# Two pairs of row-sum accumulators, and a row-sum matmul that stands one unit later

## The chip, the cores and the metric

The kernel runs on one core of a Trainium2 chip. A core has five engines with a queue each: TensorE (PE in the profile, with its weight loads as PEld), VectorE (DVE), ScalarE (ACT), GpSimd (POOL) and SyncE (SP), which here issues nearly all DMAs. An engine takes its own instructions in order and waits for others by semaphores. The metric is the device time of one launch in microseconds (us), as the median of several runs.

## The reference

The reference is four layers on one sequence of 2048 rows of 1024: attention, spectral filter, attention, spectral filter, each with a layer norm and a residual.

```python
def _A_ref(x, wqkv, wo):                     # H = 32 heads of Dh = 32
    qkv = (x @ wqkv).reshape(B, S, 3, H, Dh).transpose(2, 0, 3, 1, 4)
    q, k, v = qkv[0], qkv[1], qkv[2]
    scores = jnp.einsum("bhqd,bhkd->bhqk", q, k) * (Dh ** -0.5)
    p = softmax(scores, axis=-1)
    o = jnp.einsum("bhqk,bhkd->bhqd", p, v)
    return o.transpose(0, 2, 1, 3).reshape(B, S, D) @ wo
def _B_ref(x, w_r, w_i):
    X = rfft2(x) * (w_r + 1j * w_i)
    return irfft2(X, s=(S, D))
x = x + _A_ref(layernorm(x), wqkv, wo)
x = x + _B_ref(layernorm(x), w_r, w_i)
x = x + _A_ref(layernorm(x), wqkv, wo)
x = x + _B_ref(layernorm(x), w_r, w_i)
```

## The kernel before

**Attention.** The 32 heads are handled as 8 groups `g` of 4 heads. The loop of line 626 runs over the groups, over 4 chunks `c` of 512 queries, and over 16 key tiles `kt` of 128 keys. One step (g, c, kt) is called a unit here, and the step from kt = 15 to kt = 0 of the next chunk a chunk boundary; there are 32 chunks in each of the two attention layers.

A unit has these parts. `S` (line 552) makes the scores of 4 heads by 12 matmuls in two tiles `s` of PSUM, from a pool of three such tiles, and ScalarE turns each of them into a tile `p` of exponentials (line 562; a pool of 8 tiles). `PV` (line 564) multiplies them with V into the PSUM tile `o`; it is called at even kt for the two units before. `add` (line 575) sums the exponentials over the key tiles on VectorE, into two accumulators `acc` of 128x1024 in f32: at kt = 0 it does nothing, at kt = 1 one instruction (line 579) writes the sum of the tiles of kt = 0 and kt = 1, and from then on line 581 adds to it. So two VectorE instructions of 128x1024 belong to each unit but those of kt = 0.

`add` runs behind: the units whose PV was just issued are in `late`, and one of them is added in each of the next two units. So the last key tile of a chunk (kt = 15) is added in the unit kt = 1 of the next chunk. Right behind that stands `fin` (line 583): 4 matmuls with a matrix of ones (line 587, "the row-sum matmul" here) sum `acc` over the 128 partitions into a tile `z`, which is one of the three `s` tiles. VectorE then makes the reciprocal of it and scales the output: transpose (588), reciprocal (590), maximum into a flag (591), transpose (593), product with `oc` (594). These five are called the z instructions. At kt = 5, `out` (line 597) splits the scaled output in two f16 parts and SyncE writes it to memory.

**What sets the order.** Inside `tc.manual_schedule` (line 625) TensorE and ScalarE take their instructions in the order in which the code issues them. VectorE's and GpSimd's order, and that of the DMAs, comes from the scheduler of the framework, which sorts them by its own estimate of when they are ready.

**Filler.** Between the units of odd kt and the next, TensorE gets a piece of other work: the projections of the next groups (`qk_chunk`, line 340; `v_tiles`, line 384) or parts of the output projection (line 443). A chunk of Q or K that is complete is split by ScalarE and VectorE (lines 167 and 168), squared (344), and after four chunks `norms` (line 351) sums the squares by a small matmul (357) into another of the three `s` tiles, which VectorE reduces (359).

**Spectral layer.** `spectral` ends with 16 steps of a transpose (965), a matmul (977) and additions to x: three VectorE instructions a step (`sd` 987, and 988 and 989 into x) and one on GpSimd for two steps (992). In the first spectral layer the weights of the next attention layer are loaded beside it and split by VectorE (line 168, into `wv` and `wqk`). Line 958 opens the small pools of attention again, in memory that the constants and work tiles of the spectral layer held.

**Memory.** `acc` lies in a large tile `R` (line 203), of which attention has parts free. `open_small` (line 212) opens the pools of the attention layers one behind the other: a pool that is put in moves the addresses of those behind it.

Of the kernel before, what the change touches and what calls it, by code (L numbers as in the profile page):

```python
# [6 lines left out]
F32 = mybir.dt.float32  # L7
# [5 lines left out]
ALU = mybir.AluOpType  # L13
# [157 lines left out]
def run(g):  # L171
    for _ in g:
        pass


class Pools:
    def __init__(self, tc, side):
        self.tc, self.side, self.ctx = tc, side, ExitStack()
# [10 lines left out]
class AttnPools:  # L189


    def __init__(self, tc):
        self.tc = tc
        self.low = Pools(tc, "left")
        self.big = self.low("at_x", 1).tile([128, 16384], F32, name="big")
        self.right = Pools(tc, "right")
        r = self.right("at_r", 1).tile([128, 16384], F32, name="R")
        self.x = r.rearrange("p (t d) -> p t d", d=1024)
        k = r.bitcast(F16).rearrange("p (t a n) -> p t a n", a=2, n=2048)
        self.k = [k[:, i] for i in (3, 4, 5)]  # L200
        self.q = k[:, 2]
        v = r.rearrange("p (a t c) -> p a t c", t=16, c=128)
        self.v = [v[:, i] for i in (0, 1, 6)]
        a = r.rearrange("p (a j n) -> p a j n", j=2, n=512)
        self.acc = [a[:, i] for i in (14, 15)]

    def close(self):
        self.small.close()
# [3 lines left out]
    def open_small(self):  # L212
        small = self.small = Pools(self.tc, "left")
        self.pp = small("at_p", 8)
        self.qp = small("at_q", 1)
        self.oc = small("at_oc", 1)
        self.sgp = small("at_stage", 3)
        self.wqp = small("at_wqk", 2)
        self.wvp = small("at_wv", 1)
        self.sq = small("at_sq", 1)  # L220
        self.on = small("at_on", 2)
        self.on2 = small("at_on2", 2)
        self.sm = small("at_sm", 2)
        self.stages = [(self.sgp, "wst")] * 3 + [(self.on, "zt")] * 2 + [(self.on2, "ohl")] * 2
# [45 lines left out]
def attention(nc, tc, layer, ap, xin, yd, wts, wo, cst, dram, flags):  # L270
# [6 lines left out]
    small, psum = ap.small, Pools(tc, None)  # L277
# [118 lines left out]
    def sums(ph):  # L396
        return 8 if ph[0] == "v" else 4

    def filler():
        run(prep(phases[0]))  # L400
        for i, ph in enumerate(phases):
            nxt = prep(phases[i + 1]) if i + 1 < len(phases) else iter(())
            for n in range(sums(ph)):
                yield from (v_tiles if ph[0] == "v" else qk_chunk)(ph, n)
                for _ in range(1 + (n > 0)):
                    next(nxt, None)
            run(nxt)
# [6 lines left out]
    def load_wo():  # L414
        st = []

        def load(i):
            if i < 16:
                s = sgp.tile([128, 512], F32, name="wst")
                nc.sync.dma_start(s, wo[i // 2 * 128:i // 2 * 128 + 128, i % 2 * 512:i % 2 * 512 + 512])  # L420
                st.append(s)
        load(0)
        load(1)
        for i in range(16):
            load(i + 2)
            d, sl = i // 2, slice(i % 2 * 512, i % 2 * 512 + 512)
            split(nc, wo_t[0][d // 4][:, d % 4, sl], wo_t[1][d // 4][:, d % 4, sl], st[i], SW)
            yield
# [54 lines left out]
    def wo_parts():  # L483
        load_o(0)
        load_o(1)
        for t in [2, 3, 0, 1] + list(range(4, 12)):
            if t == 8:
                two = wvp.tile([128, 2, 1024], F32, name="wv")
                wo_dst[8], wo_dst[9] = two[:, 0], two[:, 1]
            yield from wo_part(t // 4, t % 4, wo_dst[t])  # L490
            if t in (1, 7):
                load_o(t // 4 + 2)
# [54 lines left out]
    both.clear()  # L547


    P, O, acc = {}, {}, ap.acc  # L550

    def S(g, c, kt):

        s = [psS.tile([128, 2, 512], F32, name="s") for _ in range(2)]
        for i, (a, b) in enumerate(((0, 0), (0, 1), (1, 0))):
            for h in range(4):
                r = slice(32 * h, 32 * h + 32)
                nc.tensor.matmul(s[h // 2][:, h % 2], K[g][r, a, kt * 128:kt * 128 + 128],  # L558
                                 Q[g][r, b, c * 512:c * 512 + 512], start=i == 0, stop=i == 2)
        for hf in range(2):  # L560
            p = P[g, c, kt, hf] = pp.tile([128, 2, 512], F32, name="p")
            nc.scalar.activation(p, s[hf], AF.Exp, bias=bias[g], scale=SCALE / (SQ * SQ))  # L562
# [12 lines left out]
    def add(g, c, kt):  # L575
        for hf in range(2):
            p = P[g, c, kt, hf]
            if kt == 1:
                nc.vector.scalar_tensor_tensor(acc[hf], P[g, c, 0, hf], 1e-34, p, op0=ALU.add, op1=ALU.add)  # L579
            elif kt:  # L580
                nc.vector.tensor_add(acc[hf], acc[hf], p)  # L581

    def fin(g, c):
        zt = on.tile([128, 16, 32], F32, name="zt")
        z = psS.tile([128, 2, 512], F32, name="s")[:, 0]
        for h in range(4):
            nc.tensor.matmul(z[32 * h:32 * h + 32], cst["ones"], acc[h // 2][:, h % 2], start=True, stop=True)  # L587
        nc.vector.transpose(zt.rearrange("p a b -> p (a b)"), z)
        rc = sm.tile([128, 16], F32, name="rc")
        nc.vector.reciprocal(rc, zt[:, :, 0])  # L590
        nc.vector.tensor_max(flags["r"], flags["r"], rc)
        r = on.tile([128, 512], F32, name="zt")
        nc.vector.transpose(r.rearrange("p (a b) -> p a b", b=32), rc.unsqueeze(2).broadcast_to([128, 16, 32]))
        nc.vector.scalar_tensor_tensor(r, O[g, c], SO, r, op0=ALU.mult, op1=ALU.mult)
        O[g, c] = r
# [8 lines left out]
        else:  # L604
            olast[c] = t

    pend, done, late = [], [], []
    fill, lwo, wof = filler(), load_wo(), wo_parts()
    left, parts, rests = 16, 20, list(range(12))

    def slots(f, sums, n, steps):

        while sums:
            k = max(1, int(n / sums + 0.5))
            m = -(-steps // k)
            for i in range(0, steps, m):
                while left_norms:
                    norms()
                for _ in range(min(m, steps - i)):
                    next(f, None)  # L620
                n -= 1
                yield sums - (i + m >= steps)
            sums -= 1

    with tc.manual_schedule(engines={mybir.EngineType.PE, mybir.EngineType.Activation}):
        for g in range(NG):
            todo = sum(sums(ph) for ph in beside.get(g, []))
            sl = slots(fill, todo, 22 if g == NG - 2 else 32, 24)
            wsl = slots(wof, 4, 10, 21)
            for u in range(NCH * NKT):  # L630
                c, kt = divmod(u, NKT)
                S(g, c, kt)
                if kt % 2 == 0:
                    for w in pend:
                        PV(*w)
                    late = pend
                    pend = []
                for w in late[:1]:
                    add(*w)
                    if w[2] == NKT - 1:  # L640
                        fin(*w[:2])
                        done = [w[:2]]
                late = late[1:]
                if kt == 5 and done:
                    out(*done.pop())
                pend.append((g, c, kt))
                if kt % 2 == 0:
                    continue
                if todo:
                    todo = next(sl)  # L650
                elif g == NG - 2:
                    if left:
                        run(lwo)
                        left = 0
                    if next(wsl, None) is not None and u == NCH * NKT - 1:
                        run(wsl)
                elif g == NG - 1:
                    t = rests[0] if rests else 16
                    if (t // 4 < c - 1 or t // 4 == c - 1 and kt >= 7) and (kt % 4 == 3 or not parts):
                        wo_rest(rests.pop(0))  # L660
                    elif parts:
                        parts -= 1
                        for _ in range(21):
                            next(wof)
                if g == NG - 2 and todo < 4:
                    for _ in range(2):
                        if left > (8 if todo == 3 else 0):
                            next(lwo, None)
                            left -= 1
        for w in pend:  # L670
            PV(*w)
        for w in late + pend:
            add(*w)
        run(wof)
        for t in rests:
            wo_rest(t)
# [560 lines left out]
```

## Time and profile before

| | |
|---|---|
| median of 3 runs | 3885.8 us (3885.0 to 3886.59) |
| the profiled execution's own time | 3887.92 us |
| its span, first to last instruction | 3886.0 us |
| granted TensorE clock, mean | 0.988 |
| TensorE busy | 3738.1 us (96%), 32951 instructions |
| VectorE busy | 3181.9 us (82%), 3967 instructions |
| ScalarE busy | 2901.1 us (75%), 3567 instructions |
| GpSimd busy | 304.1 us (8%), 386 instructions |
| row-sum matmul, first to last start | 175.9 to 3583.1 us |

A group row of the profile reads: line, engine, operation, what it writes <- what it reads, shape, count, then busy us in all, mean ns of one, idle us of the engine just before, and what ended that idle time. A row of the timeline reads: start us, length us, engine, line, operation, tiles, shape, how many were merged, and in brackets the engine's idle time ahead of it and what ended it. The end of a matmul is modelled, so the distance between two starts tells more of TensorE than its length. Each f32 matmul of lines 568 and 587 leaves two records. A window row reads: the stretch, its length, busy us (instructions), granted clock, share of the DMA engines, GB/s.

### The profile page before, as it was taken

The page shows a single profiled execution, that of the slowest core. Times are in us where ns is not written, and L with a number is a line of the kernel's source. Part 1 is how long each engine was busy: PE and PEld are TensorE (multiplying, and loading weights), DVE is VectorE, ACT ScalarE, POOL GpSimd, SP SyncE. Part 2 cuts the span into 40 slices and gives each one's busy share as a digit, 9 for nine tenths or more (in the row PEclk, how much of TensorE's full clock was granted, in tenths as well). Part 3 has the DMA queues.
Part 4 walks back from the last instruction along what each step waited for, and adds up shares of the span by engine and source line. Part 5 has one row for each costly group of instructions (what it writes and reads, how often), then busy time and mean ns, then how long its engine had stood idle before and what let it go on. Part 6 is the DMA issues. An engine that isn't in the chain of part 4 may idle for free.

```text
span 3886.0 us, 79635 instructions
## 1 busy us (share of the span) xinstructions
PE 3738.1 (96%) x32951; PEld 1644.2 (42%) x32951; DVE 3181.9 (82%) x3967; ACT 2901.1 (75%) x3567; POOL 304.1 (8%) x386
## 2 busy tenths in 40 slices
PE   6999999999999999989989999999999999999998
PEld 4322433343234233368854334333433432333788
DVE  6689899989998987966675998989899889788544
ACT  4578887888788865657855888888888888666686
POOL 1000000000000000014320000000000000000143
PEclk9999999999999999999999999999999999999999
DMA  8000000000000221134270000000000002111333
GB/s 204 15 12 23 12 12 17 18 12 18 12 26 7 73 70 64 62 142 140 62 179 12 15 23 12 12 18 18 12 20 12 23 12 90 53 69 66 147 99 105
DMA packets 165575, 194.08 MB, mean 50 GB/s; under 512 B 74961, under 2 KB 120657, under 8 KB 164177
## 3 DMA queue, kind: packets, MB, share of 16 engines
q1 hardware_dynamic: 164912, 188.82, 15.6%
q8 instruction: 260, 4.26, 0.5%
q14 instruction: 115, 0.93, 0.1%
q10 hardware_dynamic: 288, 0.07, 0.0%
HBM read 123.83 MB, written 48.23 MB: 44 GB/s over the span
## 4 chain that ended last, share of the span: by engine, by line
PE 73%; DVE 12%; issue 7%; ACT 3%; DMA 3%; POOL 1%; SPq 0%; DVEq 0%; ACTq 0%; POOLq 0%
PE o L568 20%; PE s L558 17%; PE x L340 12%; PE x L384 7%; PE x L443 6%; DVE R L581 3%; ACT p L562 2%; PE ps L862 2%; PE ps L800 2%; PE s L587 1%; PE ps L791 1%; DMA w<-in_w 1%; PE s L443 1%; PE o L384 1%; PE ps L977 1%
## 5 line engine op out<-in xcount | busy, mean ns | idle before, releaser
L562 ACT ACTIVATE p<-s,bias 128x1024 f32<-128x1024 f32 x2048 | 2169.7, 1112 | 575.4 <-PE s L558 564.5
L581 DVE TENSOR_TENSOR R<-R,p 128x1024 f32<-128x1024 f32 x1792 | 2089.0, 1218 | 139.4 <-ACT p L562 136.3
L568 PE MATMUL o<-p,R 128*32 128x512 f32 x8192 | 985.5, 599 | 0.0
L340 PE MATMUL x<-big,wqk 128*128 128x512 f16 x2880 | 684.2, 383 | 17.0 <-DVE Q L168 6.3
L558 PEld LDWEIGHTS <-R 32*128 32x128 f16 x12288 | 233.0, 92 | 769.3 <-issue 654.3
L340 PEld LDWEIGHTS <-wqk 128*128 128x128 f16 x3072 | 277.3, 98 | 452.9 <-issue 159.1
L558 PE MATMUL s<-Q,R 32*128 32x512 f16 x6144 | 433.0, 378 | 12.0 <-ACT p L562 10.7
L558 PE MATMUL s<-R 32*128 32x512 f16 x6144 | 432.3, 379 | 8.2 <-ACT p L562 6.7
L568 PEld LDWEIGHTS o<-p,R 128*32 128x32 f32 x8192 | 213.8, 109 | 524.6 <-issue 524.0
L384 PEld LDWEIGHTS <-big 128*128 128x128 f16 x3072 | 296.5, 100 | 155.5 <-issue 73.9
L384 PE MATMUL x<-wv,big 128*128 128x256 f16 x2688 | 324.1, 277 | 34.5 <-DMA big<-hl 34.5
L579 DVE SCALAR_TENSOR_TENSOR R<-p 128x1024 f32<-128x1024 f32 x128 | 153.9, 1203 | 196.1 <-ACT p L562 195.7
L443 PE MATMUL x<-big 128*128 128x512 f16 x1050 | 237.4, 380 | 0.0
L365 POOL PARTITION_ALL_REDUCE mall<-mqk x16 | 40.7, 2542 | 2333.8 <-DVE mqk L359 2322.5
L443 PEld LDWEIGHTS <-big 128*128 128x128 f16 x1344 | 126.2, 98 | 178.0 <-issue 34.6
L910 DVE TENSOR_TENSOR H<-G,H 128x512 f16<-128x512 f32 (+1 forms) x68 | 46.5, 683 | 105.4 <-ACT H L909 105.3
L862 PE MATMUL ps<-cbi,H 128*128 128x256 f16 (+1 forms) x792 | 99.2, 273 | 6.0 <-ACT H L909 3.7
L855 ACT COPY U<-ps 64x256 f32<-64x256 f32 (+1 forms) x272 | 97.2, 357 | 8.4 <-PE ps L862 3.3
L855 ACT COPY B<-ps 64x256 f32<-64x256 f32 (+1 forms) x272 | 97.1, 357 | 6.7 <-PE ps L862 2.4
L862 PE MATMUL ps<-cb,big 128*128 128x256 f16 x780 | 96.3, 273 | 0.0
L805 DVE TENSOR_TENSOR big<-ps,big 128x512 f16<-128x512 f32 x64 | 44.5, 695 | 58.5 <-ACT big L804 58.5
L167 ACT ACTIVATE R<-x 128x512 f16<-128x512 f32 x88 | 52.7, 598 | 50.5 <-PE x L340 50.4
(429 smaller groups left out, 2992.5 us busy)
## 6 DMA issues: line engine op xcount, KB each, us to landing
wst<-in_wp SPq DMA_DIRECT2D x96, 256.0 KB, 3.0
R<-y SPq DMA_DIRECT2D x32, 512.0 KB, 5.4
w<-in_w SPq DMA_DIRECT2D x60, 256.0 KB, 2.7
od<-ohl SPq DMA_DIRECT2D x56, 256.0 KB, 2.4
big<-od SPq DMA_DIRECT2D x16, 896.0 KB, 6.7
y<-R SPq DMA_DIRECT2D x20, 512.0 KB, 2.7
R<-in_x SPq DMA_DIRECT2D x16, 512.0 KB, 5.8
wst<-in_wo SPq DMA_DIRECT2D x32, 256.0 KB, 3.0
```

Source lines behind the costliest of these rows:

```text
L167: nc.scalar.activation(hi, src, AF.Copy, scale=scale)
L340: nc.tensor.matmul(ps, a, b, start=d == 0 and i == 0, stop=d == 7 and i == 2)
L384: nc.tensor.matmul(ps[:, j], l, r, start=d == 0 and i == 0, stop=d == 7 and i == 2)
L443: nc.tensor.matmul(p, a, b, start=start and d == ds[0] and i == 0, stop=stop and d == ds[-1] and i == 2)
L558: nc.tensor.matmul(s[h // 2][:, h % 2], K[g][r, a, kt * 128:kt * 128 + 128], Q[g][r, b, c * 512:c * 512 + 512], start=i == 0, stop=i == 2)
L562: nc.scalar.activation(p, s[hf], AF.Exp, bias=bias[g], scale=SCALE / (SQ * SQ))
L568: nc.tensor.matmul(O[g, c][32 * h:32 * h + 32], V[g][:, kt, 32 * h:32 * h + 32], P[g, c, kt, h // 2][:, h % 2], start=kt == 0, stop=kt == ...
L579: nc.vector.scalar_tensor_tensor(acc[hf], P[g, c, 0, hf], 1e-34, p, op0=ALU.add, op1=ALU.add)
L581: nc.vector.tensor_add(acc[hf], acc[hf], p)
L800: nc.tensor.matmul(pa[:, j], tt[:, j], mm[:, g], start=True, stop=True)
L855: nc.scalar.copy(ov[64 * r:64 * r + 64, a0:a0 + m, x], tl[64 * x:64 * x + 64, :m, r])
L862: nc.tensor.matmul(out, l, r, start=k == 0, stop=k == len(mm_) - 1)
```

## The change

Even chunks keep the accumulators in `R`. Odd chunks get a second pair, `acc1`, in a new pool of 8 KB a partition that opens behind `at_p`. The last `add` of a chunk no longer calls `fin`; it leaves the chunk in `full`, and `fin` is called in the unit kt = 2, behind the `PV` calls for kt = 0 and kt = 1. `out` stays at kt = 5. Memory that the program reserves for DMA descriptors is set to 4096 bytes a partition.

```diff
@@ class AttnPools
-        self.acc = [a[:, i] for i in (14, 15)]
+        self.acc0 = [a[:, i] for i in (14, 15)]
@@ def open_small
         self.pp = small("at_p", 8)
+        self.accp = small("at_acc", 1)
         self.qp = small("at_q", 1)
@@ def attention
-    P, O, acc = {}, {}, ap.acc
+    P, O = {}, {}
+    acc1 = ap.accp.tile([128, 2, 2, 512], F32, name="acc")
+    acc = [ap.acc0, [acc1[:, i] for i in range(2)]]
@@ def add
         for hf in range(2):
             p = P[g, c, kt, hf]
+            t = acc[c % 2][hf]
             if kt == 1:
-                nc.vector.scalar_tensor_tensor(acc[hf], P[g, c, 0, hf], 1e-34, p, op0=ALU.add, op1=ALU.add)
+                nc.vector.scalar_tensor_tensor(t, P[g, c, 0, hf], 1e-34, p, op0=ALU.add, op1=ALU.add)
             elif kt:
-                nc.vector.tensor_add(acc[hf], acc[hf], p)
+                nc.vector.tensor_add(t, t, p)
@@ def fin
-            nc.tensor.matmul(z[32 * h:32 * h + 32], cst["ones"], acc[h // 2][:, h % 2], start=True, stop=True)
+            nc.tensor.matmul(z[32 * h:32 * h + 32], cst["ones"], acc[c % 2][h // 2][:, h % 2], start=True, stop=True)
@@ the loop over units
-    pend, done, late = [], [], []
+    pend, done, late, full = [], [], [], []
...
                     late = pend
                     pend = []
+                    if kt == 2 and full:
+                        done = [full.pop()]
+                        fin(*done[0])
                 for w in late[:1]:
                     add(*w)
                     if w[2] == NKT - 1:
-                        fin(*w[:2])
-                        done = [w[:2]]
+                        full = [w[:2]]
@@ def kernel
-    nc = _bacc.Bacc("TRN2", target_bir_lowering=False, num_devices=1)
+    nc = _bacc.Bacc("TRN2", target_bir_lowering=False, num_devices=1, dynamic_dma_scratch_size=4096)
```

What it moves is shown at three places. In the changed kernel the lines are 561 for S, 571 for PV, 591 for the row-sum matmul, 341 for the filler, 583 and 585 for the sums, 592 to 598 for the z instructions and 993 to 995 for the spectral additions.

TensorE at the start of chunk 1 of group 2, second attention layer (`s` is the scores, `x` the filler's sum); before, the row-sum matmul stands between the last matmul of S of kt = 1 and the filler:

```order
L558 MATMUL s<-R 128x512
L587 MATMUL s<-R,ones 32x512 x4
L340 LDWEIGHTS wqk
L340 MATMUL x<-big,wqk 128x512
L340 LDWEIGHTS wqk
```

and now, with the 8 matmuls of the two PV of unit kt = 2 ahead of it:

```order
L561 MATMUL s<-R 128x512
L571 MATMUL o<-p,R 32x512 x8
L591 MATMUL s<-R,ones 32x512 x4
L561 LDWEIGHTS R
L561 MATMUL s<-R 128x512
```

It moved behind the filler, S of kt = 2 and the 8 matmuls of PV, and S of kt = 3 follows it. The three `s` tiles are taken in turn, so the tile of `z` is next wanted by S of kt = 4, where before it was wanted by S of kt = 3.

VectorE at the same boundary, before (`zt` and `rc` belong to the z instructions, line 168 and 344 are the split and the square of a chunk of K):

```order
L579 SCALAR_TENSOR_TENSOR R<-p 128x1024
L588 STREAM_TRANSPOSE zt<-s 128x512
L579 SCALAR_TENSOR_TENSOR R<-p 128x1024
L590 RECIPROCAL rc<-zt 128x16
L168 SCALAR_TENSOR_TENSOR R<-x,R 128x512
L591 TENSOR_TENSOR fr<-fr,rc 128x16
L593 STREAM_TRANSPOSE zt<-rc 128x512
L344 TENSOR_TENSOR sq<-R 128x512
L594 SCALAR_TENSOR_TENSOR zt<-oc,zt 128x512
L581 TENSOR_TENSOR R<-R,p 128x1024 x8
```

and now at the same boundary (the chunk that begins is odd, so its sums go to `acc`; the first row is its sum of kt = 0 and kt = 1, both halves):

```order
L583 SCALAR_TENSOR_TENSOR acc<-p 128x1024 x2
L168 SCALAR_TENSOR_TENSOR R<-x,R 128x512
L345 TENSOR_TENSOR sq<-R 128x512
L585 TENSOR_TENSOR acc<-acc,p 128x1024 x2
L592 STREAM_TRANSPOSE zt<-s 128x512
L594 RECIPROCAL rc<-zt 128x16
L595 TENSOR_TENSOR fr<-fr,rc 128x16
L597 STREAM_TRANSPOSE zt<-rc 128x512
L598 SCALAR_TENSOR_TENSOR zt<-oc,zt 128x512
L585 TENSOR_TENSOR acc<-acc,p 128x1024 x6
```

The five z instructions stand together now, behind the additions of kt = 2; before, other instructions lay between them. Nothing else of VectorE's order in the attention loops moved, but that at six boundaries the reduction of line 359 stands ahead of the first sum of the chunk.

VectorE at the end of the first spectral layer, before (`wv` and `wqk` are the weights being split):

```order
L987 TENSOR_TENSOR sd<-e,ps 128x512
L989 TENSOR_TENSOR R<-R,ps 128x16x8x4
L168 SCALAR_TENSOR_TENSOR wv<-wst,wv 128x4x128
L988 TENSOR_TENSOR R<-R,ps 128x16x8x4
L987 TENSOR_TENSOR sd<-e,ps 128x512
L989 TENSOR_TENSOR R<-R,ps 128x16x8x4
L168 SCALAR_TENSOR_TENSOR wv<-wst,wv 128x4x128
L168 SCALAR_TENSOR_TENSOR wqk<-wst,wqk 128x512
L987 TENSOR_TENSOR sd<-e,ps 128x512
L988 TENSOR_TENSOR R<-R,ps 128x16x8x4
L168 SCALAR_TENSOR_TENSOR wqk<-wst,wqk 128x512
```

and now:

```order
L993 TENSOR_TENSOR sd<-e,ps 128x512
L995 TENSOR_TENSOR R<-R,ps 128x16x8x4
L168 SCALAR_TENSOR_TENSOR wv<-wst,wv 128x4x128 x2
L993 TENSOR_TENSOR sd<-e,ps 128x512
L994 TENSOR_TENSOR R<-R,ps 128x16x8x4
L168 SCALAR_TENSOR_TENSOR wqk<-wst,wqk 128x512
L995 TENSOR_TENSOR R<-R,ps 128x16x8x4
L994 TENSOR_TENSOR R<-R,ps 128x16x8x4
L993 TENSOR_TENSOR sd<-e,ps 128x512
L995 TENSOR_TENSOR R<-R,ps 128x16x8x4
L168 SCALAR_TENSOR_TENSOR wqk<-wst,wqk 128x512
```

The splits of weights moved against the steps: the new pool shifts the tiles that the loads go to, so they wait for other work. A GpSimd addition (line 992, now 998) starts behind every second step's `sd`. ScalarE's order differs at one such split, and those of GpSimd and SyncE are the same; some of their waits name other engines.

## Prediction

> **What bounds the kernel now.** I read the page first: busy shares, then the chain of work that ended last. In each of the two rows the reader should look at how far TensorE stands above VectorE.
>
> ```profile
> PE 3738.1 (96%) x32951; PEld 1644.2 (42%) x32951; DVE 3181.9 (82%) x3967; ACT 2901.1 (75%) x3567; POOL 304.1 (8%) x386
> PE 73%; DVE 12%; issue 7%; ACT 3%; DMA 3%; POOL 1%; SPq 0%; DVEq 0%; ACTq 0%; POOLq 0%
> ```
>
> TensorE is busy for 96% of the span and carries 73% of the chain; VectorE carries 12% of it, so there are stretches where VectorE sets the pace. Next come the groups of instructions, for the two lines around the change:
>
> ```profile
> L579 DVE SCALAR_TENSOR_TENSOR R<-p 128x1024 f32<-128x1024 f32 x128 | 153.9, 1203 | 196.1 <-ACT p L562 195.7 <-PE s L587 0.5
> L587 PE MATMUL s<-R,ones 128*32 128x512 f32 x512 | 73.9, 604 | 1.6 <-DVE R L581 1.4 <-ACT p L562 0.2
> ```
>
> VectorE's idle time ahead of the first sum of a chunk is 195.7 us on ScalarE's exponentials and only 0.5 us on the row-sum matmul. That is the first warning: the write-after-read wait which a second pair of accumulators takes away costs VectorE almost nothing. The row-sum matmul runs 64 times, 73.9 us in all. An undisturbed one, at 2485.02 below, shows 1.06, and 64 of those are 67.8; so TensorE lost 6.1 us inside and 1.6 ahead, 7.7 us in all, by waiting for the last additions. Then the timeline at one quiet boundary (chunk 1 of group 2, second attention layer), where the reader follows the starts of TensorE and of VectorE:
>
> ```profile
> 2484.26 0.83 PE L558 MATMUL s<-R 32*128 32x512 f16 x12
> ...
> 2485.02 1.06 PE L587 MATMUL s<-R,ones 128*32 128x512 f32 x8
> ...
> 2486.01 1.90 PE L340 MATMUL x<-big,wqk 128*128 128x512 f16 x8
> 2486.27 1.23 DVE L579 SCALAR_TENSOR_TENSOR R<-p 128x1024 f32<-128x1024 f32 x1 [2.04 <-ACT p L562]
> 2487.41 0.71 DVE L588 STREAM_TRANSPOSE zt<-s 128x512 f32<-128x512 f32 x1
> ...
> 2487.85 0.83 PE L558 MATMUL s<-R 32*128 32x512 f16 x12
> ...
> 2488.05 1.18 DVE L579 SCALAR_TENSOR_TENSOR R<-p 128x1024 f32<-128x1024 f32 x1
> 2488.60 1.92 PE L568 MATMUL o<-p,R 128*32 128x512 f32 x16
> ...
> 2489.15 0.24 DVE L590 RECIPROCAL rc<-zt 128x16 f32<-128x16 f32 x1
> 2489.31 0.63 DVE L168 SCALAR_TENSOR_TENSOR R<-x,R 128x512 f16<-128x512 f32 x1
> ...
> 2489.86 0.16 DVE L591 TENSOR_TENSOR fr<-fr,rc 128x16 f32<-128x16 f32 x1
> 2489.93 0.70 DVE L593 STREAM_TRANSPOSE zt<-rc 128x512 f32<-128x512 f32 x1
> ...
> 2490.46 0.83 PE L558 MATMUL s<-R 32*128 32x512 f16 x12
> 2490.56 0.38 DVE L344 TENSOR_TENSOR sq<-R 128x512 bf16<-128x512 f16 x1
> 2490.86 0.68 DVE L594 SCALAR_TENSOR_TENSOR zt<-oc,zt 128x512 f32<-128x512 f32 x1
> ...
> 2491.46 9.16 DVE L581 TENSOR_TENSOR R<-R,p 128x1024 f32<-128x1024 f32 x8
> ```
>
> TensorE has no gap here; the row-sum matmul takes 0.99 from its start to the next one, and no wait stands in brackets on TensorE. VectorE waits 2.04 for exponentials and then works without a pause. At other boundaries TensorE does wait:
>
> ```profile
> 726.83 2.35 DVE L581 TENSOR_TENSOR R<-R,p 128x1024 f32<-128x1024 f32 x2
> 728.19 2.09 PE L587 MATMUL s<-R,ones 128*32 128x512 f32 x8 [0.56 <-DVE R L581]
> 729.34 1.23 DVE L579 SCALAR_TENSOR_TENSOR R<-p 128x1024 f32<-128x1024 f32 x1 [0.16 <-PE s L587]
> ...
> 732.79 0.69 DVE L168 SCALAR_TENSOR_TENSOR R<-x,R 128x512 f16<-128x512 f32 x1 [0.33 <-ACT R L167]
> ```
>
> The matmul starts 0.56 late and then its second half waits for the second addition, 1.03 more (2.09 against 1.06). I went through all 64 in this way: seven waits make up the 7.7 us, six in the first attention layer. What matters is what VectorE does next. For each boundary I took the stretch from its first sum to the next place where TensorE waits for VectorE, or to where VectorE runs dry, and asked for VectorE's busy time. For 22 boundaries the stretch ends in a TensorE wait; first, last and sum are:
>
> ```profile
> 177.20:200.80 23.60, 23.52 (x28) 1.00 0.04 12
> ...
> 3250.60:3291.50 40.90, 40.76 (x50) 0.96 0.49 162
> sum 545.70, DVE 540.52; mean DVE 24.57
> ```
>
> VectorE is busy 540.52 of 545.70 us, 99%. So at these 22, to which all seven boundaries belong, VectorE is the bound until the stretch ends; a wait of TensorE that is removed at its start is met again at its end.
>
> **The change, part by part.** Profiled execution and median stand 2.1 us apart (3887.9 against 3885.8); I make the sum against the profiled one and subtract it from the median alike.
>
> *The waits at the old place.* 7.7 us go there and come back behind, but for what VectorE itself idled: 0.16 and 0.33 in the rows above, at the three boundaries where it idles so (the others show none), 0.49 x 3 = 1.5. **-1.5** (ends: 0, and -7.7 if all stays gone).
>
> *The matmul joins a run of PV.* Alone, 8 records take 0.99. PV's 16 records of the same kind take 2490.46 - 2488.60 = 1.86, eight more than the 0.99 of eight alone: the second eight cost 0.87, so joining a run saves 0.12. It is worth something where TensorE is the bound: 64 matmuls, of which 2 stand behind the last chunk of a layer and are not moved, less 22, is 40. **-4.8** (ends: 0 and 62 x 0.12 = -7.4).
>
> *The reduction of norms.* At six boundaries a small matmul follows that takes the next `s` tile:
>
> ```profile
> 317.90 1.07 PE L587 MATMUL s<-R,ones 128*32 128x512 f32 x8
> 319.17 0.40 PE L357 MATMUL s<-sq,bones 128*32 128x512 bf16 x4 [0.20 <-ACT p L562]
> ```
>
> It starts 1.27 behind the row-sum matmul in place of 0.99, as the tile is still being read by ScalarE. With `z` gone from there it gets the tile that `z` had: 0.28 x 6. **-1.7** (ends: 0, and -1.7).
>
> *VectorE's order.* The five z instructions stand in a row now. Before, others lay between, and a row's start came ahead of the end of the one before: 2488.05 is 0.07 ahead of 2487.41 + 0.71. Neighbours of which one needs the other's result do not overlap so:
>
> ```profile
> 826.15 0.70 DVE L593 STREAM_TRANSPOSE zt<-rc 128x512 f32<-128x512 f32 x1
> 826.89 0.69 DVE L594 SCALAR_TENSOR_TENSOR zt<-oc,zt 128x512 f32<-128x512 f32 x1
> ```
>
> The second starts 0.04 behind the end of the first. At 2487.41 the five took, start to next start, 0.64 + 0.16 + 0.07 + 0.63 + 0.60 = 2.10. In a row I take 0.75 + 0.28 + 0.07 + 0.74 + 0.60 = 2.44, the durations plus 0.04 at the three dependent neighbours: 0.34 more. That is free where VectorE has slack and whole where it is the bound, at 22: **+7.5** (ends: 0, and 22 x 0.46 = +10.1 if the fourth pair waits too). [...]
>
> *The buffer.* `z` leaves the `s` pool later; S of kt = 4 wants its tile, before S of kt = 3. Counting from S of kt = 1 at 2484.26, TensorE now runs S 0.76, filler 1.84, S 0.75, PV 1.86, z 0.87, S 0.75, filler 1.84: S of kt = 4 is wanted at +8.67. VectorE's first sum starts at +2.01; two sums 2.3, split 0.6, square 0.3, two additions 2.3 (row 726.83), transpose 0.71: the tile is free at +8.2. Half a microsecond of room. **0** in the forecast; its failing is rival C.
>
> *End of the first spectral layer.* The new pool moves addresses, and splits of weights change places against GpSimd's additions. A split that meets one is slow:
>
> ```profile
> 1925.63 0.67 DVE L168 SCALAR_TENSOR_TENSOR wv<-wst,wv 128x512 f16<-128x512 f32 x1
> 1928.42 3.10 POOL L992 TENSOR_TENSOR R<-R,sd 128x1024 f32<-128x1024 f32 x1 [13.90 <-DVE sd L987]
> 1928.86 3.21 DVE L168 SCALAR_TENSOR_TENSOR wv<-wst,wv 128x512 f16<-128x512 f32 x1
> ...
> 1947.90 2.02 PE L977 MATMUL ps<-mi,tt 128*128 128x128 f32 x16 [1.12 <-DVE R L988]
> ```
>
> 3.21 against 0.67, 2.5 each. Three stand behind such a start before and two now; TensorE waits for VectorE there only 1.12. I take half. **-1.3** (ends: 0 and -2.5).
>
> *More accumulators, smaller descriptor memory, later loads:* no instruction is added, and SyncE's order is the same; 0.
>
> The sum is -1.5 - 4.8 - 1.7 + 7.5 - 1.3 = **-1.8**: 3886.1 on the profiled execution, 3884.0 against the median.
>
> **The rivals.** *A, VectorE does not bound those stretches:* the seven waits go for good and the chain of z costs nothing: -7.7 - 4.8 - 1.7 - 1.3 = -15.5, 3870.3. The 73.9 in the group row speaks for it; the 99% against.
>
> *B, the row of z instructions costs nothing:* if VectorE's next row waits for the last one's end in any case, the forecast less 7.5, 3876.5. For it: within the chain of the trace only one dependent pair of neighbours could be read. Against: its row. [...]
>
> *C, the end on the other side: `z` holds its `s` tile too long.* If one more addition (1.22) gets ahead of the transpose, the tile comes free at +9.4, and with ScalarE's exponentials behind S pushed too, S of kt = 4 waits 0.7 to 1.1, say 0.9. The boundaries where filler of Q and K adds a split and a square to VectorE are about 20 of the 40: +18 on the forecast, 3902 (3894 to 3910). It decides as soon as the transpose ends later than 8.67 behind S of kt = 1. For it: half a microsecond is small beside the 2.04 by which VectorE's start depends on exponentials. Against: in the order only the two additions of kt = 2 precede it.
>
> **How the numbers follow.** Forecast 0.60, A 0.10, B 0.12, C 0.18. The likeliest one is 3884.0; its own range is 3877 to 3894, the first with the VectorE term at 0, the second with TensorE's gains at 0 and VectorE's at its upper end (3885.8 + 10.1 - 1.5, rounded). What a measurement of this kernel can tell from no change is about 0.2%, 7.8 us: 3878.0 to 3893.6. The forecast lies within it, A and B are faster, C slower: faster 0.22, same 0.60, slower 0.18. For 8 in 10 the range takes in B with 2 us below it and the cheaper part of C: 3874 to 3900; A and the dearer part of C, about 0.10 each, are left out.
>
> **What would show it.** In the changed profile the row-sum matmul's row should fall from 73.9 to about 62 with no idle on VectorE's additions, while TensorE's waits on line 168's, 345's and 359's results in the first attention layer grow by about as much as went. The product with `oc` should start 0.04 behind the end of its transpose; if ahead, B. S of kt = 4 with a wait on a z transpose in brackets means C, and busy VectorE well under 99% in the 22 stretches means A. What would make all of it wrong is a wait that I haven't seen in TensorE's order: the row-sum matmul itself now stands ahead of S of kt = 3, so if VectorE's last addition ends behind PV, every exponential behind it is late.

## The result and the profile after

| | before | changed |
|---|---|---|
| median of 20 runs each | 3886.3 us (3882.0 to 3893.3) | 3889.0 us (3883.1 to 3893.7) |
| ratio | | 1.0004, 95% interval 0.9998 to 1.0011 |
| the profiled execution's span | 3886.0 us | 3888.7 us |
| TensorE busy | 3738.1 us | 3726.9 us |
| VectorE busy | 3181.9 us | 3192.0 us |

The ratio is +1.6 us, between -0.8 and +4.3: no change that this measurement can tell, where -1.8 was forecast. The page of the changed kernel, busy times first, then the groups that answer to those shown of before (the row-sum matmul has two rows now, one for each pair), with the two on which TensorE waits for VectorE:

```profile
PE 3726.9 (96%) x32951; PEld 1649.8 (42%) x32951; DVE 3192.0 (82%) x3967; ACT 2897.0 (74%) x3567; POOL 304.3 (8%) x386
L341 PE MATMUL x<-big,wqk 128*128 128x512 f16 x2880 | 685.0, 384 | 24.5 <-DVE Q L168 11.2 <-DVE R L168 5.6 <-ACT wqk L167 5.4
L591 PE MATMUL s<-acc,ones 128*32 128x512 f32 x256 | 33.4, 593 | 0.0
L591 PE MATMUL s<-R,ones 128*32 128x512 f32 x256 | 33.3, 592 | 0.0
L358 PE MATMUL s<-sq,bones 128*32 128x512 bf16 x128 | 18.9, 391 | 17.3 <-DVE sq L345 16.0 <-POOL sq L345 1.0 <-ACT p L565 0.4
```

and the two waiting groups of the kernel before, which the prediction did not show:

```profile
L340 PE MATMUL x<-big,wqk 128*128 128x512 f16 x2880 | 684.2, 383 | 17.0 <-DVE Q L168 6.3 <-ACT wqk L167 5.4 <-DVE R L168 3.2
L357 PE MATMUL s<-sq,bones 128*32 128x512 bf16 x128 | 15.6, 389 | 10.7 <-DVE sq L344 8.1 <-ACT p L562 1.6 <-POOL sq L344 1.0
```

The row-sum matmul waits for nothing any more and is down from 73.9 + 1.6 to 66.7 us. The filler's wait grew from 17.0 to 24.5, the wait of the sum of squares from 10.7 to 17.3. Added over the two attention layers, TensorE's idle times of more than 0.1 us that VectorE ended were 23.6 us in 26 waits (1.4 of it at the row-sum matmul, whose wait for the second addition stands inside its rows) and are 42.9 us in 55.

Where it went was read by laying the two traces side by side. TensorE's order is the same but for the row-sum matmul, so each group of matmuls has its partner, and the difference of their start times is a running account. One chunk as an example: S of kt = 1 at two chunk boundaries in a row, before and then changed.

```profile
2484.26 0.83 PE L558 MATMUL s<-R 32*128 32x512 f16 x12
...
2528.72 0.83 PE L558 MATMUL s<-R 32*128 32x512 f16 x12
```

```profile
2485.97 0.83 PE L561 MATMUL s<-R 32*128 32x512 f16 x12
2486.72 1.90 PE L341 MATMUL x<-big,wqk 128*128 128x512 f16 x8
...
2491.05 1.04 PE L591 MATMUL s<-R,ones 128*32 128x512 f32 x8
2492.03 0.83 PE L561 MATMUL s<-R 32*128 32x512 f16 x12
...
2508.95 0.38 PE L358 MATMUL s<-sq,bones 128*32 128x512 bf16 x1 [0.16 <-DVE sq L345]
...
2530.91 0.83 PE L561 MATMUL s<-R 32*128 32x512 f16 x12
```

The chunk took 44.46 before and 44.94 now, 0.49 more by unrounded times: the matmul's place saves 0.14, and behind it TensorE waits for VectorE. By starts the account grows by 0.54 at the sum of squares, of which the row at 2508.95 shows 0.16 as idle time since the end of a matmul is modelled, and by 0.1 behind it, where S waits for the reduction of line 360. In the second attention layer these accounts repeat to 0.01 us from group to group, so they say more than the total. 25 boundaries of that layer fall into five kinds (A to E are names for this text): A, into chunk 1 of a group (7 of them); B, into chunk 2 of groups 0, 2 and 4, where the filler is 12 matmuls (3); C, the others of groups 0 to 5, with no wait for VectorE behind them (9); D, into chunk 0 of groups 2, 4 and 6 (3); E, into chunk 0 of groups 1, 3 and 5, with the reduction of the norms (3). The start of the layer and the six boundaries from chunk 2 of group 6 on are left out. Time of the chunk that follows, in us against before, for the changed kernel and the experiments below, each from one trace:

| kernel | A | B | C | D | E |
|---|---|---|---|---|---|
| changed | +0.49 | +0.56 | -0.14 | +0.13 | -0.15 |
| two pairs, old place | 0.00 | +0.01 | 0.00 | 0.00 | 0.00 |
| two pairs, old place, z instructions in a row | +0.34 | +0.15 | 0.00 | 0.00 | 0.00 |
| changed, z between the additions | 0.00 | +0.57 | -0.14 | +0.13 | -0.15 |
| changed, z between, one addition later | +0.18 | +0.86 | -0.14 | +0.42 | +0.14 |
| matmul ahead of PV, z mostly in a row | +0.34 | +0.41 | -0.14 | -0.03 | -0.30 |
| matmul ahead of PV, z between | -0.01 | +0.57 | -0.14 | +0.12 | -0.15 |
| matmul ahead of PV, z between, first one early | -0.01 | -0.06 | -0.14 | -0.14 | -0.41 |

The account of the changed kernel by stages: start +0.2, first attention layer +3.5, first spectral layer -3.1, second attention layer +3.0, end -0.5; 3.1 at the last group of TensorE, of which 2.7 remain at the end of the span.

### The profile page after: what moved, and what is told of

Same layout as the page of the kernel before. It is cut to its first block, busy times and chain, and to the rows that moved or that the text cites. A ratio compares the mean times of both kernels' runs of the same rounds, so it can differ in the third digit from the quotient of the medians.

```text
span 3888.7 us, 79508 instructions
## 1 busy us (share of the span) xinstructions
PE 3726.9 (96%) x32951; PEld 1649.8 (42%) x32951; DVE 3192.0 (82%) x3967; ACT 2897.0 (74%) x3567; POOL 304.3 (8%) x386
## 4 chain that ended last, share of the span: by engine, by line
PE 40%; DVE 6%; issue 5%; ACT 2%; DMA 1%; POOL 1%; DVEq 0%; POOLq 0%; SPq 0%; ACTq 0%
PE o L571 10%; PE s L561 8%; PE x L341 6%; PE x L385 4%; PE x L444 3%; PE ps L868 2%; PE ps L806 2%; DMA w<-in_w 1%; PE s L444 1%; PE ps L797 1%; PE ps L983 1%; DVE acc L585 1%; DVE R L585 1%; ACT p L565 1%; PE ps L971 1%
## 5 line engine op out<-in xcount | busy, mean ns | idle before, releaser
L585 DVE TENSOR_TENSOR R<-R,p 128x1024 f32<-128x1024 f32 x896 | 1043.0, 1219 | 69.3 <-ACT p L565 68.7
L585 DVE TENSOR_TENSOR acc<-acc,p 128x1024 f32<-128x1024 f32 x896 | 1046.7, 1219 | 62.9 <-ACT p L565 61.5
L341 PE MATMUL x<-big,wqk 128*128 128x512 f16 x2880 | 685.0, 384 | 24.5 <-DVE Q L168 11.2
L444 PEld LDWEIGHTS <-big 128*128 128x128 f16 x1344 | 126.2, 98 | 174.1 <-issue 30.7
L583 DVE SCALAR_TENSOR_TENSOR R<-p 128x1024 f32<-128x1024 f32 x64 | 75.6, 1222 | 112.0 <-ACT p L565 112.0
L583 DVE SCALAR_TENSOR_TENSOR acc<-p 128x1024 f32<-128x1024 f32 x64 | 75.7, 1222 | 66.1 <-ACT p L565 66.1
```

The source lines that it names most:

```text
L341: nc.tensor.matmul(ps, a, b, start=d == 0 and i == 0, stop=d == 7 and i == 2)
L444: nc.tensor.matmul(p, a, b, start=start and d == ds[0] and i == 0, stop=stop and d == ds[-1] and i == 2)
L583: nc.vector.scalar_tensor_tensor(t, P[g, c, 0, hf], 1e-34, p, op0=ALU.add, op1=ALU.add)
L585: nc.vector.tensor_add(t, t, p)
```

## The experiments

**Second pair alone.** Two pairs and the smaller descriptor memory stay, the row-sum matmul goes back into the last addition:

```diff
-                    if kt == 2 and full:
-                        done = [full.pop()]
-                        fin(*done[0])
...
-                        full = [w[:2]]
+                        fin(*w[:2])
+                        done = [w[:2]]
```

> Changed kernel with the row-sum matmul put back into the last addition of a chunk (two pairs of accumulators and the smaller descriptor memory stay). My theory: the second pair buys nothing by itself, VectorE waited 0.5 us in all for the row-sum matmul; so the attention layers take the time they took before, within 1.5 us, and only the end of the first spectral layer gains some 3 us: about 3883 against 3886 of before. Rival, the second pair frees VectorE for the next chunk: the waits of TensorE on line 168's results get shorter, 5 us or more below before.

Measured 3879.1, ratio 0.9981 (0.9972 to 0.9990). In the second attention layer the table shows 0.00: there the second pair buys nothing. The first layer gained 4.4, which I had not expected; 0.9 and 1.5 of it stand behind 386.47 and 980.86 of before, where TensorE did not fall to half clock this time (before it is granted 0.50 from 386.64 and from 980.56; see the last section). So neither theory is fully right: VectorE's wait is worth nothing, and still the kernel is 7.5 us faster. The trace cannot be added up to these 7.5, as it is of the fastest of the eleven runs, 14.1 us shorter than that of before; its largest pieces are the first layer's 4.4, 2.65 from the end of the first spectral layer and 1.8 from the start. What makes up the rest of the 7.5 stays open.

**Memory alone.**

```diff
+        self.accp = small("at_acc", 1)
...
+    acc1 = ap.accp.tile([128, 2, 2, 512], F32, name="acc")
...
-    nc = _bacc.Bacc("TRN2", target_bir_lowering=False, num_devices=1)
+    nc = _bacc.Bacc("TRN2", target_bir_lowering=False, num_devices=1, dynamic_dma_scratch_size=4096)
```

> Kernel before with the new pool opened and a tile taken from it that nothing uses, and the descriptor memory at 4096 bytes; one pair of accumulators, old place. My theory: the attention layers take what they took, to 0.1 us a chunk; the end of the first spectral layer and the start of the next attention layer gain about 3 us: 3883. Rival, those 3 us are a difference between one profile and the next: 3886, and the profile's times of the spectral additions as before.

Measured 3882.1, ratio 0.9990 (0.9981 to 0.9999). Between 1915 and 1985 us of before, the end of the first spectral layer, it gains 2.64; the changed kernel gains 2.63 there, and the second layer is 0.0 a chunk. In both, 0.3 of it is lost again at the next group, 1985.5, so that 2.3 remain. The gain is there without any change of order in the source; the next run tells the addresses from the smaller descriptor memory.

**The pool behind the others.** The changed kernel, with `at_acc` opened last, so that the others keep their addresses:

```diff
         self.pp = small("at_p", 8)
-        self.accp = small("at_acc", 1)
...
         self.sm = small("at_sm", 2)
+        self.accp = small("at_acc", 1)
```

> Changed kernel with the new pool opened behind all the other small pools, so that their addresses are those of before. Theory: the end of the first spectral layer gains nothing (0 within 0.5 us from 1930 to 1985 where the changed kernel and the one with the pool alone gained 2.4 to 2.6), and the second attention layer is as in the changed kernel; 2 to 3 us above it. Rival, the smaller descriptor memory or chance gave the 2.4: the gain is there again.

In one run 3891.5, and 0.28 in place of 2.63 in that stretch (0.0 in place of 2.3 behind 1985.5). The group of TensorE that waits there, in the kernel before, then the changed one, then with the pool last:

```profile
L977 PE MATMUL ps<-mi,tt 128*128 128x128 f32 x512 | 62.3, 275 | 1.6 <-DVE R L988 1.6
```

```profile
L983 PE MATMUL ps<-mi,tt 128*128 128x128 f32 x512 | 62.1, 275 | 0.3 <-DVE R L994 0.3
```

```profile
L983 PE MATMUL ps<-mi,tt 128*128 128x128 f32 x512 | 62.3, 275 | 1.6 <-DVE R L994 1.6
```

The wait comes back with the addresses. So do the slow splits: three that meet an addition of GpSimd take 3.1 to 3.2 us before and with the pool last, and two do so in the changed kernel. The smaller descriptor memory is in this kernel too, so it is not the cause.

**One pair, new place.**

```diff
-    acc = [ap.acc0, [acc1[:, i] for i in range(2)]]
+    acc = [ap.acc0, ap.acc0]
```

> Changed kernel with one pair of accumulators for all chunks, so the first sum of a chunk waits until the moved row-sum matmul has read them. My theory: the first sum starts 4 us later at each boundary (row-sum matmul done 6.2 us behind S of kt = 1 in place of 2.0), and this is paid in full where VectorE is the bound: 22 to 33 boundaries, 92 to 139 us, 3980 to 4028. Rival, the 8 tiles of exponentials hide it: below 3900.

Measured 4051.5, ratio 1.0425 (1.0409 to 1.0441): 165 us, more than the 92 to 139 expected.

```profile
L583 DVE SCALAR_TENSOR_TENSOR R<-p 128x1024 f32<-128x1024 f32 x128 | 154.1, 1205 | 273.3 <-PE s L591 236.4 <-ACT p L565 36.9
```

VectorE waits 236.4 us for the row-sum matmul, 3.7 a boundary, and pays at more boundaries than my 22 to 33. The mean granted clock is 0.974 in place of 0.988, so a part of the 165 that was not taken apart is half clock (see the last section), which the expectation had not counted. The second pair is what makes the new place possible; it is no gain of its own.

**The five z instructions in a row, at the old place.** `fin` issues only the matmuls here, and `fin_step(k)` the z instructions: 0 the transpose, 1 the reciprocal, 2 the flag and the second transpose, 3 the product. Edges of order (`inline`, here and below) put each of them, and the additions beside them, behind the one before on VectorE. Here they follow both first sums of the chunk, with reciprocal, flag, second transpose and product in a row:

```diff
+        if kt == 1:
+            for k in range(4):
+                fin_step(k)
```

> Two pairs of accumulators, row-sum matmul at its old place, but the z instructions stand behind both first sums with reciprocal, flag and second transpose in a row. Theory, the row is what costs: in the second attention layer each boundary where VectorE is the bound loses 0.2 to 0.4 against the same kernel without the row (which shows 0.00 against before), 2 to 4 us in that layer. Rival, the place on TensorE is what costs: 0.0 at these boundaries.

One run, 3892.7. A shows +0.34 where the same kernel without the row shows 0.00, B +0.15; the layer is 2.4 us longer than before, where without the row it is 0.7 shorter (all of it in one chunk, where before falls to half clock, 0.50 from 3274.32, and that kernel does not). Only VectorE's order differs between these two. At A VectorE idles in neither between its first sum and the additions, so that the later place of the transpose leaves no gap there. The row costs, also at the old place.

**The five between the additions.** The z instructions stand behind the additions of kt = 2 and kt = 3, one step after each; TensorE as changed:

```diff
-                nc.vector.tensor_add(t, t, p)
+                i = nc.vector.tensor_add(t, t, p)
+                if "w" in Z or line:
+                    inline(i)
+            if kt in (2, 3):
+                fin_step(2 * kt - 4 + hf)
```

> Changed kernel with the five z instructions put between the additions of kt = 2 and kt = 3 on VectorE, one after each, by order edges; TensorE's order is that of the changed kernel. My theory, the price of the change is that the five stand in a row: 0.4 to 0.5 us go at each of 22 boundaries, 0.27 at 11 more, and the two stretches at half clock behind TensorE's longest waits: 14 to 17 us below the changed kernel, 3872 to 3875. Rival, the price is the new place on TensorE (S of kt = 3 and all exponentials behind it start later): no gain, 3887 to 3890.

Measured 3873.7, ratio 0.9969 (0.9957 to 0.9982). A falls from +0.49 to 0.00. But B and D do not move, so the row is not the whole price.

**One addition later.**

```diff
-            if kt in (2, 3):
-                fin_step(2 * kt - 4 + hf)
+            for k in {5: (0,), 6: (1, 2), 7: (3,)}.get(2 * kt + hf, ()):
+                fin_step(k)
```

> As the kernel with the z instructions between the additions, but with the first of them behind both additions of kt = 2, and one addition of kt = 3 behind it and one ahead of the last. In the kernel with them between, VectorE still idled 0.37 for the row-sum matmul at the boundaries with 12 filler matmuls. Theory, price is VectorE's idle and its chain: those boundaries (+0.57 there) come to about 0.2 or less, the others stay within 0.15 of it; 3872 to 3875. Rival, TensorE's place sets +0.57 there: it stays at +0.57.

Measured 3884.0, ratio 0.9995 (0.9986 to 1.0004). My theory fell: B went up to +0.86, D to +0.42, E to +0.14. The wait for the row-sum matmul (0.37) that I took for B's cause was not it. Two things came with the later place: at B VectorE now idles 0.16 and 0.48 for exponentials, and reciprocal, flag and second transpose stand in a row again. This run does not tell one from the other.

**The matmul ahead of PV,** with VectorE's order left to the scheduler, which put the first transpose between the additions of kt = 2 and the other four in a row:

```diff
                 if kt % 2 == 0:
+                    if kt == 2 and full:
+                        done = [full.pop()]
+                        fin(*done[0])
                     for w in pend:
                         PV(*w)
```

> Changed kernel with the row-sum matmul ahead of the two PV of kt = 2 in place of behind them. Theory: on TensorE the same 0.14 is saved per boundary; VectorE gets its transpose 1.9 us earlier, between the two additions of kt = 2, so one dependent neighbour less and no idle for it: +0.2 to +0.4 in place of +0.49 at the boundaries where VectorE is the bound, and less than +0.57 at those with 12 filler matmuls. Rival, any place behind the filler costs the same: +0.49 and +0.57.

One run, 3882.4. As expected: 0.14 still saved at C, A at +0.34, B at +0.41.

**The same, z between the additions; and with the first of them ahead of the additions of kt = 2.** The second differs from the first in this:

```diff
-            if kt in (2, 3):
-                fin_step(2 * kt - 4 + hf)
+            if 3 <= 2 * kt + hf <= 6:
+                fin_step(2 * kt + hf - 3)
```

> The same, but the first z instruction stands behind the first addition of kt = 2, as in the kernel with them between. Theory: VectorE's idle for the row-sum matmul, 0.37 at the boundaries with 12 filler matmuls, is gone, since the matmul comes 1.9 us earlier, but the 0.16 for exponentials stays: those boundaries cost 0.1 to 0.3 in place of 0.57; the others as in the kernel with the earlier first z instruction. 3870 to 3878.

> Row-sum matmul ahead of the two PV of kt = 2, and the five z instructions between the additions of kt = 2 and kt = 3, the first of them ahead of these additions, so it can fill VectorE's idle time for exponentials. Theory, the price has two parts, dependent neighbours in a row and z work that came too late to fill that idle time: both go, while the 0.12 to 0.14 of TensorE stay: in the second attention layer 0.0 to 0.1 at the boundaries that cost 0.49, 0.0 to 0.2 at those that cost 0.56, -0.15 or lower at all others, 2 to 3 us below before in that layer; 3869 to 3876 in all. Rival, only the row matters: the boundaries that cost 0.56 stay at 0.4 or more, as with the z instructions between the additions at the changed kernel's place.

The first measured 3872.4, ratio 0.9969 (0.9956 to 0.9981), with B still at +0.57, against my expectation. The second measured 3863.1, ratio 0.9945 (0.9932 to 0.9959), below the 3869 to 3876 expected, B at -0.06, D at -0.14 and E at -0.41. VectorE at the same boundary of kind B shows why. First between:

```profile
2520.46 2.36 DVE L583 SCALAR_TENSOR_TENSOR R<-p 128x1024 f32<-128x1024 f32 x2 [3.44 <-ACT p L565]
...
2523.34 0.42 DVE L345 TENSOR_TENSOR sq<-Q 128x512 bf16<-128x512 f16 x1
2523.92 1.23 DVE L585 TENSOR_TENSOR R<-R,p 128x1024 f32<-128x1024 f32 x1 [0.16 <-ACT p L565]
2525.07 0.71 DVE L612 STREAM_TRANSPOSE zt<-s 128x512 f32<-128x512 f32 x1
...
2527.39 1.23 DVE L585 TENSOR_TENSOR R<-R,p 128x1024 f32<-128x1024 f32 x1 [0.35 <-ACT p L565]
```

and with the first transpose ahead of the additions:

```profile
2514.20 2.36 DVE L583 SCALAR_TENSOR_TENSOR R<-p 128x1024 f32<-128x1024 f32 x2 [3.44 <-ACT p L565]
...
2517.08 0.42 DVE L345 TENSOR_TENSOR sq<-Q 128x512 bf16<-128x512 f16 x1
2517.54 0.72 DVE L612 STREAM_TRANSPOSE zt<-s 128x512 f32<-128x512 f32 x1
2518.18 1.18 DVE L585 TENSOR_TENSOR R<-R,p 128x1024 f32<-128x1024 f32 x1
2519.28 0.24 DVE L615 RECIPROCAL rc<-zt 128x16 f32<-128x16 f32 x1
2519.45 1.16 DVE L585 TENSOR_TENSOR R<-R,p 128x1024 f32<-128x1024 f32 x1
```

Between, VectorE idles 0.16 and 0.35 for exponentials of the new chunk and is then busy until TensorE waits for it. With the transpose, 0.72 long, ahead of the additions it does z work in that time and idles no more at this place. That is the second part of the price: the z instructions filled a time in which VectorE had nothing else. Moved later, they leave it empty and are still to be done. This kernel beats both: TensorE's 0.14 a boundary and the 0.28 of the norms are kept, and VectorE pays nothing at A and B. Most of its gain stands elsewhere, though: its trace is 19.6 us shorter than that of before, of which 3.4 are in the second attention layer, 11.4 in the first, with two stretches at half clock fewer, and 4.2 between them. The first layer's part was not taken apart.

**Less work for VectorE.**

```diff
-            elif kt:
+            elif kt and kt != 4:
                 nc.vector.tensor_add(t, t, p)
```

> Changed kernel that leaves out the two additions of kt = 4 in each chunk: 2.3 us less for VectorE, its row sums lack one key tile. Theory, VectorE is the bound of the stretches behind the boundaries: TensorE's waits on VectorE, 42.9 us in 55 waits in the attention layers of the changed kernel, fall below 15, and the boundaries that cost 0.49 and 0.57 turn to -0.14 or lower: 25 to 35 us faster than the changed kernel. Rival, these waits come from late exponentials: they stay above 30 us.

One run, 3861.3, 27.6 us below the changed kernel. In the second layer TensorE's waits for VectorE fall from 12.2 us to 1.5, A turns from +0.49 to -0.67 (groups 0, 2, 4, 6) and -1.78 (the others), B to -0.24, D to -0.14: VectorE was the bound there. In the first layer they fall only from 30.7 to 25.0, so the 15 us expected were missed. There VectorE waits for loads of weights as well, and takes its work in another order, as in this row of the kernel with fewer additions:

```profile
737.70 0.69 DVE L261 TENSOR_REDUCE wm<-wst 128x1 f32<-128x512 f32 x1 [2.37 <-DMA wst<-in_wp]
```

How much of the first layer's 25.0 us these loads make was not measured.

## Why the prediction was right, and where it was not

The total was right: no change that can be told, inside the range, and the forecast's case. Its terms were less good, and their errors partly cancel, so that the total is in part luck. By the traces' account, term by term:

*The waits at the old place* (-1.5 after coming back) and *VectorE's order* (+7.5) were to make +6.0 at the 22 boundaries where VectorE is the bound; they made +10.4. Of this 2.4 is half clock at two of them (granted 0.50 from 615.47 and from 755.41, where before is granted 1.00), and before had itself lost some 0.7 to half clock at another one, into chunk 2 of group 6 of the second layer (0.50 from 3274.32; the two pairs at the old place show -0.68 there); without the clock it is about +8.7. The mechanism was right: the seven waits went, and TensorE waits behind. The signs were coarser than the forecast had them: the row-sum matmul's rows fell to 66.7, not to about 62, and TensorE's other waits on VectorE grew by more than the 7.7 that went, from 18.0 to 30.7 us in the first attention layer and from 4.1 to 12.2 in the second. The size was too small at +0.34 a boundary: it measured +0.49 at A and +0.56 at B. VectorE at the example boundary in the changed kernel:

```profile
2487.97 2.36 DVE L583 SCALAR_TENSOR_TENSOR acc<-p 128x1024 f32<-128x1024 f32 x2 [2.03 <-ACT p L565]
2490.25 0.68 DVE L168 SCALAR_TENSOR_TENSOR R<-x,R 128x512 f16<-128x512 f32 x1
2490.85 0.42 DVE L345 TENSOR_TENSOR sq<-R 128x512 bf16<-128x512 f16 x1
2491.18 2.35 DVE L585 TENSOR_TENSOR acc<-acc,p 128x1024 f32<-128x1024 f32 x2
2493.45 0.71 DVE L592 STREAM_TRANSPOSE zt<-s 128x512 f32<-128x512 f32 x1
2494.20 0.25 DVE L594 RECIPROCAL rc<-zt 128x16 f32<-128x16 f32 x1
2494.49 0.17 DVE L595 TENSOR_TENSOR fr<-fr,rc 128x16 f32<-128x16 f32 x1
2494.58 0.70 DVE L597 STREAM_TRANSPOSE zt<-rc 128x512 f32<-128x512 f32 x1
2495.32 0.69 DVE L598 SCALAR_TENSOR_TENSOR zt<-oc,zt 128x512 f32<-128x512 f32 x1
2495.93 6.90 DVE L585 TENSOR_TENSOR acc<-acc,p 128x1024 f32<-128x1024 f32 x6
```

The five take 2.48 from 2493.45 to 2495.93, against 2.10 before: 0.38. The three dependent neighbours start 0.04 behind an end, as the rows had said. The other 0.11 is in the sums, the split and the square, which ran in 2.28 + 0.60 + 0.33 here and in 1.14 + 1.10 + 0.55 + 0.30 before, where short z instructions stood beside them; the step that bounded the term by the z instructions alone left that out. At B idle time for exponentials comes to the row, 0.16 ahead of the additions of kt = 2, where before shows none between the first sum and the additions: the step "chain of z, whole where VectorE is the bound" took for granted that VectorE would be as busy at the start of the stretch as before.

*The matmul joins a run of PV:* -0.12 forecast, -0.14 measured at C and in every kernel with the new place. What failed is the step that counted 40 boundaries as TensorE's. At D and E the filler's next wait for line 168 comes back with 0.27, so the 40 and the norms together gave -3.9 in place of -6.5. *The reduction of norms* is the same failure: the 0.28 was gained at its place (1.27 became 0.99, less the wait) and lost 16 us later. With the z instructions early it stays: -0.41 at E.

*End of the first spectral layer:* the mechanism was right, the size was half: -2.63 measured (-2.3 with what the next group loses again), -1.3 taken. The prediction read one wait of 1.12 there; the row of line 977 above shows 1.6, as a second one of 0.48 follows at 1954.55, and the prediction halved the gain as well.

*Rivals.* A (waits gone for good) is out: 42.9 us of waits. C (the `s` tile) is out as S of kt = 4 goes: TensorE's waits on a z transpose come to 0.2 us in the whole group of S:

```profile
L561 PE MATMUL s<-Q,R 32*128 32x512 f16 x6144 | 431.3, 377 | 9.9 <-ACT p L565 8.7 <-DVE mqk L360 1.0 <-DVE zt L592 0.2
L444 PE MATMUL s<-big,ohl 128*128 128x512 f16 x186 | 45.2, 380 | 3.0 <-DVE zt L592 3.0
```

The second row shows C's mechanism at another place: in the last group of each layer the output projection takes its tile from the same pool, and behind four boundaries it waits 0.75 for the z transpose, 3.0 in all, where before has no such wait. It cost next to nothing, as at the same places S waited 0.48 for exponentials before: the running account moves by 0.05 at each.

B (a row of dependent instructions costs nothing) is out by the row at the old place, +0.34 against 0.00. In the changed kernel's rows of VectorE above, a next instruction that needs no result of the one before starts up to 0.09 us ahead of its end (2491.18 against 2490.85 + 0.42), and one that does, 0.04 behind (2494.20 against 2493.45 + 0.71).

## What to carry to other kernels

A wait that is removed at the start of a stretch in which another engine is the bound is met again at its end; ask where the stretch ends before booking it. Work that is moved later on an engine may have been filling a time in which that engine had nothing to do: look at what its idle time will wait for when the work is gone, and put it back in the gap. Of a chain of short dependent instructions, one independent instruction between each two hid what the dependence costs on VectorE here (A from +0.49 to 0.00).

## What the runs showed of the hardware

TensorE's clock fell to half for 3.41 us behind some of its waits of some 2 us, and not behind others. Granted clock (the number ahead of the DMA share) of two such stretches in the kernel before, and one behind an equal wait:

```profile
386.64:390.05 3.41, 3.41 (x20) 2.16 (x22) 3.41 (x5) 0.00 (x0) 0.94 (x1) 0.50 0.00 0
1120.51:1123.92 3.41, 3.41 (x15) 2.10 (x15) 3.41 (x4) 0.00 (x0) 0.48 (x1) 0.50 0.00 0
614.52:617.93 3.41, 3.41 (x24) 1.29 (x23) 3.41 (x4) 0.20 (x1) 0.00 (x0) 1.00 0.00 0
```

The waits ahead of them, 1.95, 1.90 and 1.95 us:

```profile
386.16 0.38 PE L357 MATMUL s<-sq,bones 128*32 128x512 bf16 x1 [1.95 <-DVE sq L344]
...
1120.49 0.59 PE L357 MATMUL s<-sq,bones 128*32 128x512 bf16 x1 [1.90 <-DVE sq L344]
```

```profile
614.52 2.75 PE L340 MATMUL x<-big,wqk 128*128 128x512 f16 x12 [1.95 <-DVE Q L168]
```

In the changed kernel the third wait is 2.96, and half clock follows it, 0.50 from 615.47 to 618.88:

```profile
615.00 4.43 PE L341 MATMUL x<-big,wqk 128*128 128x512 f16 x12 [2.96 <-DVE Q L168]
```

4.43 for the 12 matmuls in place of 2.75: 1.7 us for one such stretch. From chunk 0 of group 0 to the end of the first layer there are four in the kernel before, six in the changed one, two in the fastest. In the traces of the kernel before and the changed one all of them begin at multiples of 3.413 us from each other (before: 130.64, 246.70, 386.64, 980.56 and 1120.51, which are 34, 41, 174 and 41 steps apart; changed: 246.83, 386.77, 615.47, 755.41, 984.11 and 1124.05, which are 41, 67, 41, 67 and 41 apart), and the one at 130.64 before lies at 130.77 in the changed kernel. By the multiples above all three waits lie whole inside one step of 3.413 us, the third in that from 611.92 to 615.34, so the phase alone does not tell the two that brought half clock from the one that did not; what does stays open. From 140 to 3600 us, less the stretch from 1660 to 2100, TensorE idled 1.78, 1.90, 1.95, 1.95 and 2.15 us in the steps just ahead of half clock in the kernel before, and 2.73 to 3.41 in the six of the changed kernel. No half clock followed steps with 1.95 and 1.58 of idle time before, nor any with less (up to 1.41 before, up to 1.36 in the changed kernel). Whether the phase of these steps makes up the spread of several us between runs of one kernel was not tested.
